# Late modulation weights of an adaLN block: other rooms for them, and their loads earlier in SyncE's list

## The chip, the cores and the metric

One core of a Trainium2 chip runs the whole program in one launch. The metric is the device time of the core in microseconds. TensorE (PE) multiplies, VectorE (DVE), ScalarE (ACT) and GpSimd (POOL) do the elementwise work, and SyncE (SP) issues nearly all DMAs. Each engine works through its own list of instructions in order; an instruction that has to wait holds up all that stand behind it on that engine.

## The reference, cut to what matters

```
mod = silu(c) @ w_mod                      # 640 -> 6 x 640: sa, ca, ga, sb, cb, gb
h = layernorm(x) * (1 + ca) + sa
x = x + ga * S4(h)                         # kernel of 2048 taps from the SSM parameters, FFT convolution, + h * Dskip
h = layernorm(x) * (1 + cb) + sb
x = x + gb * SwiGLU(h)                     # w1, w3: 640 x 1728, w2: 1728 x 640
```

x is 2048 x 640. The matrix `w_mod` has 3840 columns. The first 1920 (sa, ca, ga) are needed early, for the input and the kernel of the convolution. The last 1920 (sb, cb, gb) are the **late modulation weights**: their results are first used after the convolution.

## The kernel before, in words

The program has three parts. A **front** (the first 120 us or so) computes the SSM parameters, the early modulation, the layer norm of all 16 row tiles of x and the first step of the convolution's transform of the input (called u). Then **rounds** generate the convolution kernel for 40 groups of channels and run the rest of the transforms. Then the two branches of the **SwiGLU** run as large matrix products.

The front is ordered by a table of words written by hand, `FRONT`. Each word is one step, and the engines receive their instructions in the order of the words; the steps are kept in that order on each engine. The words that matter here:

- `um+j`: PE transforms row tile j into two tiles of PSUM. The first of them, with tag Z, is the only one of its kind.
- `ua+j`, `ub+j`: DVE (or ACT, with `/s`) copies the two halves into the SBUF tile `u` of row tile j. There are two such tiles, so `ua+15` (or `ub+14`, the first of its pair for row tile 14) writes where row tile 13 (or 12) was, and has to wait until that one is stored.
- `us+j`: SP stores tile `u` to DRAM, 128 rows of 1280 numbers, 640 KB. `us+12` is the thirteenth store.
- `wl+i`: SP loads late modulation weights i, 384 columns, 960 KB, in one or two DMAs.
- `qs+i`: PE multiplies them, in a PSUM tile with tag Z; `qp+i`, `qc+i`, `qv+i` bring the result into place (`mod_part`, `late_turn`, `late_cols`).
- `ul+0`: SP loads the first part of u back from DRAM. It waits for all stores of u.

In the order of the table, `qs+0` stands behind `ua+15`, since both use the PSUM tile with tag Z.

The five loads go into **rooms**: pieces of the large tile `uk` that hold other things at other times. `uk` has three planes of 4096 numbers per partition. `w_room(f, i, n, pitch)` gives the room that begins at number `i * pitch` of plane f, so each plane has two rooms for late weights, (f, 0) and (f, 1). Before, plane 0 holds the SSM parameters (`prm`: A, B, C, later their products), plane 2 holds temporary values of the same computation (`ldt`, `dt`, `m0` in its first room; `t3`, `gr`, `gi` and `l2` in its second). The steps of that computation on channels 128 to 639 are the words `d0` to `dN`; the last that touch the rooms are `dM`, `dN` (the phase, from `m0` and two of the products), `dA` (`dt` and `t3`) and `dB` (A's imaginary part and `t3`), all on DVE, and `dK` on PE (`l2`).

All loads and stores named here are issued by SP through one queue. Beside what a DMA's data needs, SP waits before it for the completion of the DMA that used the same completion semaphore before; eight such semaphores (`DMAHW0` to `DMAHW7`) take turns.

## Time and profile before

| | us |
|---|---|
| three runs | 929.12 median (928.58 to 930.3) |
| the profiled execution | 927.25, of which the span 925.5 |
| busy in the span: PE, DVE, ACT, POOL | 887.9, 698.9, 548.6, 265.9 |

The granted TensorE clock is 1.00 in all 40 slices of the span. The span is the time from the first to the last instruction of the profiled execution; 1.75 us of its run lie outside. PE is busy for 96% of the span, DVE for 76%. The change lies between 88 us and 121 us, in the last quarter of the front; what an engine waits for there has to be read from that stretch.

### The profile page before, as it was taken

What the parts mean: (1) busy time and instruction counts of PE and PEld (TensorE: products, weight loads), DVE (VectorE), ACT (ScalarE), POOL (GpSimd) and SP (SyncE); (2) the same over time, 40 slices, a digit from 0 to 9 for tenths busy, and PEclk for the clock granted to TensorE, in tenths of its full rate; (3) what the DMA queues carried; (4) which work ended last, traced back from release to release, by engine and by line L of the source; (5) the groups of instructions that cost most, each with busy time, mean ns of one, the idle gap of its engine ahead of it and who ended that gap; (6) DMA issues with size and microseconds to landing.
All of it is one profiled execution on the core that took longest, in us unless ns stands there. A gap on an engine that the chain in (4) does not pass through costs nothing.

```text
span 925.5 us, 21047 instructions
## 1 busy us (share of the span) xinstructions
PE 887.9 (96%) x8461; PEld 692.2 (75%) x8461; DVE 698.9 (76%) x1250; ACT 548.6 (59%) x811; POOL 265.9 (29%) x278
## 2 busy tenths in 40 slices
PE   5999889999999998999999999999999999999998
PEld 3776567777777666678888887778888888888886
DVE  6799888999999967876666655686976666664665
ACT  4899899999999743564343323556633333333432
POOL 3633454445446330243222201210522222100000
PEclk9999999999999999999999999999999999999999
DMA  8755898655656887942131217974322211103452
GB/s 254 258 202 192 272 226 216 176 161 157 178 159 174 200 264 213 261 176 86 57 111 60 58 44 217 278 234 153 95 64 71 85 58 57 58 29 100 150 177 101
DMA packets 103765, 140.68 MB, mean 152 GB/s; under 512 B 20212, under 2 KB 62964, under 8 KB 103668
## 3 DMA queue, kind: packets, MB, share of 16 engines
q1 hardware_dynamic: 100108, 129.48, 46.9%
q0 software_dynamic: 2048, 7.34, 2.4%
q10 hardware_dynamic: 1512, 2.52, 0.8%
q8 instruction: 66, 1.08, 0.5%
q14 instruction: 31, 0.25, 0.1%
HBM read 107.85 MB, written 31.46 MB: 151 GB/s over the span
## 4 chain that ended last, share of the span: by engine, by line
PE 67%; ACT 14%; DVE 12%; DMA 4%; issue 2%; SPq 0%; POOL 0%; DVEq 0%; ACTq 0%; POOLq 0%
PE ps L111 58%; ACT A L145 3%; PE p L676 3%; ACT ph L145 2%; ACT cs L145 2%; DVE E L597 2%; ACT L145 2%; DVE uk L111 2%; PE pm L111 1%; DVE A L604 1%; ACT kc L148 1%; PE pt L637 1%; DVE E L600 1%; ACT uk L148 1%; DMA A<-zs 1%
## 5 line engine op out<-in xcount | busy, mean ns | idle before, releaser
L111 DVE TENSOR_TENSOR s<-ps,s 128x512 f32<-128x512 f32 x138 | 95.0, 688 | 80.1 <-PE ps L111 79.8
L570 POOL TENSOR_TENSOR ph<-thi,iota 128x1024 int32<-128x1024 int32 x40 | 86.0, 2150 | 142.3 <-DVE A L608 94.9
L111 DVE TENSOR_TENSOR gl<-rw,gh 128x640 fp32r<-128x640 f32 x87 | 78.1, 897 | 64.3 <-ACT gh L111 64.3
L111 ACT CAST gh<-rw 128x640 fp32r<-128x640 f32 x87 | 63.2, 727 | 100.4 <-PE ps L111 62.6
L111 PE MATMUL ps<-xA,gh 128*128 128x512 f32 x280 | 88.5, 393 | 0.1
L111 PE MATMUL ps<-gh,uh 128*128 128x512 f32 x224 | 87.5, 390 | 0.0
L111 PE MATMUL ps<-gl,uh 128*128 128x512 f32 x224 | 87.2, 389 | 0.0
L111 POOL TENSOR_TENSOR S<-rw 128x256 f32<-128x256 f32 x46 | 36.5, 795 | 174.1 <-DVE S0l L111 163.1
L676 PE MATMUL p<-uk,s 128*64 128x256 f32 x640 | 77.9, 385 | 6.8 <-DVE Y L701 2.4
L111 PE MATMUL ps<-gh,ul 128*128 128x512 f32 x208 | 81.1, 390 | 0.0
L676 PEld LDWEIGHTS p<-uk,s 128*64 128x64 f32 x640 | 44.6, 136 | 29.5 <-DVE Y L701 3.5
L111 PEld LDWEIGHTS ps<-xA,gh 128*128 128x128 f32 x280 | 52.2, 188 | 13.6 <-issue 1.0
L111 PE MATMUL ps<-xA,gl 128*128 128x512 f32 x140 | 54.5, 390 | 0.0
L604 DVE TENSOR_TENSOR A<-A,ph 128x1024 f32<-128x1024 f32 x40 | 51.8, 1295 | 0.0
L111 ACT ACTIVATE s<-ps 128x512 f32<-128x512 f32 (+1 forms) x33 | 19.7, 597 | 53.1 <-PE ps L111 53.1
L597 DVE TENSOR_TENSOR E<-A,cs 128x1024 f32<-128x1024 f32 x40 | 50.2, 1254 | 0.6 <-ACT A L145 0.6
L111 PEld LDWEIGHTS ps<-gl,uh 128*128 128x128 f32 x224 | 42.1, 188 | 9.0
L111 PEld LDWEIGHTS ps<-gh,uh 128*128 128x128 f32 x224 | 42.1, 188 | 8.8
L111 PEld LDWEIGHTS ps<-gh,ul 128*128 128x128 f32 x208 | 39.0, 188 | 8.4
L574 POOL TENSOR_TENSOR ph<-ph,phi 128x512 int32<-128x512 int32 x40 | 44.5, 1115 | 2.5
L727 PE MATMUL pz<-Y,i 64*128 64x128 f32 x640 | 44.4, 278 | 0.7 <-ACT h L148 0.4
L727 PEld LDWEIGHTS pz<-Y,i 64*128 64x128 f32 x640 | 38.9, 187 | 7.1 <-issue 5.8
(251 smaller groups left out, 2287.8 us busy)
## 6 DMA issues: line engine op xcount, KB each, us to landing
rw<-in_w_dram SPq DMA_DIRECT2D x52, 320.0 KB, 2.9
us<-u SPq DMA_DIRECT2D x16, 640.0 KB, 3.2
s<-in_s_dram SPq DMA_DIRECT2D x40, 256.0 KB, 4.8
i<-in_i_dram SPq DMA_DIRECT2D x40, 256.0 KB, 3.3
rw<-in_wg_dram SPq DMA_DIRECT2D x31, 320.0 KB, 3.9
rw<-in_wu_dram SPq DMA_DIRECT2D x28, 320.0 KB, 2.8
uk<-us SPq DMA_DIRECT2D x32, 256.0 KB, 4.6
zs<-zt SPq DMA_DIRECT2D x16, 512.0 KB, 4.8
```

Of the source, the lines that this page charges most:

```text
L111: ins = fn(*args, **kw)
L145: return tc.keep_in_program_order(S.activation(*args, **kw))
L148: return tc.keep_in_program_order(S.copy(out, in_))
L570: keep(G.tensor_tensor(p, bc(thi[:, s * SD:s * SD + SD], 2, NPH), bc(iota, 1, SD), op=OP.mult))
L574: keep(G.tensor_tensor(p[:, :, :NA], p[:, :, :NA], bc(phi[:, s * SD:s * SD + SD], 2, NA), op=OP.add))
L597: keep(V.tensor_tensor(EC[s][:, :, 1:3, :], AA[s][:, :, 1:3, :], mid(cs[s]), op=OP.mult))
L600: keep(V.tensor_tensor(EC[s][:, :, 0, :], AA[s][:, :, 0, :], cs[s][:, :, 2 * NA - 1:NA - 1:-1], op=OP.mult))
L604: keep(V.tensor_tensor(A[:, :, 1:3, :], A[:, :, 1:3, :], mid(ph[s]), op=OP.mult))
L637: keep(PE.matmul(pt[c * 64:c * 64 + 64, g, :], kk[:, g, :], s1[:, c, :], start=True, stop=True, tile_position=(0, c * 64)))
L676: keep(PE.matmul(p2[par * 64:par * 64 + 64, pi, c, :], s2[:, pi * 2 + par, c * 64:c * 64 + 64], uk[:, 0:kn + 1:kn, f, :], start=True, stop ...
L727: ins = keep(PE.matmul(pz[:, par, (g % 2) * 2 + pi, :], i1[r, pi, c, :], Y[r, pi, c, :], start=(c == 0), stop=(c == 1), tile_position=(par ...
```

## The change

`late_load` gets another table of rooms. Loads 1 and 3 exchange their rooms: load 1 goes to (0, 1) where it was (2, 1), load 3 to (2, 1) where it was (0, 1). Loads 0, 2 and 4 keep theirs. In the table, `wl+0` and `wl+1` move in front of `us+12`, and also in front of the step `dB`; `wl+2` moves in front of `us+13`; `wl+3` moves from behind `um+15` to right behind `us+13`; `wl+4` stays.

```diff
-        wl[i] = w_load(w_room(0 if i in (2, 3) else 2, i % 2, WC, 2048), 1920 + i * WC)
+        wl[i] = w_load(w_room(*((2, 0), (0, 1), (0, 0), (2, 1), (2, 0))[i], WC, 2048), 1920 + i * WC)
...
-        "uk+0 ub+11/s dJ PI+7 kg+4 ua+11/s us+10 lg+7 dK/2 dN ln+12 lv+7 dA dH AB+7 um+12/A E1+6 dL us+11 dB "
-        "ua+12/s pt+2 SI+6 A1+5 uk+2 ub+12 us+12 K+4 um+13/B/2 ub+13 ua+13 ln+15 E2+5 ln+14 A1+6 wl+0 CO+7 "
+        "uk+0 ub+11/s dJ PI+7 kg+4 ua+11/s us+10 lg+7 dK/2 dN ln+12 lv+7 dA dH AB+7 um+12/A E1+6 dL us+11 wl+0 wl+1 dB "
+        "ua+12/s pt+2 SI+6 A1+5 uk+2 ub+12 us+12 wl+2 K+4 um+13/B/2 ub+13 ua+13 ln+15 E2+5 ln+14 A1+6 CO+7 "
```

This is the piece of SP's list that differs. The first row kept on both sides belongs to `us+10`, the second to `us+11`; the other rows `us<-u` are `us+12` and `us+13`; a row `uk<-in_w_mod_dram` is one DMA of a late load (384 columns: loads 0 and 4; 96 and 288: load 1; 192 twice: load 2; 288 and 96: load 3). In brackets stands what SP waits for.

```order
 L111 DMA us<-u 128x1280 [waits DMAHW0_49,DVE_49,Activation_49]
 L111 DMA us<-u 128x1280 [waits DMAHW1_49,Activation_49]
-L111 DMA us<-u 128x1280 [waits DMAHW2_49,DVE_49,Activation_49]
-L111 DMA uk<-in_w_mod_dram 128x5x384 [waits DMAHW3_49,Pool_49]
-L111 DMA us<-u 128x1280 [waits DMAHW4_49,DVE_49]
+L111 DMA uk<-in_w_mod_dram 128x5x384 [waits DMAHW2_49,DVE_49,Pool_49]
+L111 DMA uk<-in_w_mod_dram 128x5x96 [waits DMAHW3_49]
+L111 DMA uk<-in_w_mod_dram 128x5x288 [waits DMAHW4_49]
+L111 DMA us<-u 128x1280 [waits DMAHW5_49,DVE_49,Activation_49]
+L111 DMA uk<-in_w_mod_dram 128x5x192 [waits DMAHW6_49]
```

Between `us+11` and `us+12` there is now load 0 and load 1, three DMAs, and between `us+12` and `us+13` load 2, two DMAs, where load 0 stood. Load 0 now waits for DVE itself.

On DVE no instruction moves. This is the piece of its list around the evictions of row tiles 14 and 15; the rows `u<-pu,shift` with a change are `ub+14` and `ua+15`, which wait for the stores of row tiles 12 and 13.

```order
-L111 TENSOR_TENSOR u<-pu,shift 128x640 [waits DMAHW2_49,PE_49]
+L111 TENSOR_TENSOR u<-pu,shift 128x640 [waits DMAHW5_49,PE_49]
 L111 TENSOR_TENSOR u<-pu,shift 128x640
 L625 TENSOR_TENSOR pk<-pk,dz 128x4 [waits PE_49]
...
-L111 TENSOR_TENSOR u<-pu,shift 128x640 [waits DMAHW4_49,PE_49]
+L111 TENSOR_TENSOR u<-pu,shift 128x640 [waits DMAHW0_49,PE_49]
```

The same two stores are waited for; only their semaphores are others, since the stores stand at other places in SP's list. PE, ACT and POOL keep their instructions and their order too.

## Rows read from the trace of the kernel before

**Rows 1.** The page's chain of work that ended last, shares by engine

```profile
PE 67%; ACT 14%; DVE 12%; DMA 4%; issue 2%; SPq 0%; POOL 0%; DVEq 0%; ACTq 0%; POOLq 0%
```

**Rows 2.** Pieces of that chain, 93 to 116 us: start us, us, what

```profile
97.70 7.38 DMA us<-u
...
105.17 0.84 DVE u L111
...
106.05 1.02 PE pm L111 x16
...
113.69 0.45 PE pq L556 x4
...
114.15 0.93 ACT A L145 x2
```

**Rows 3.** Waits, 90 to 150 us: engine, line, releaser: total us, times, longest

```profile
ACT A L145 <- PE pa L545: 2.6, 3, 1.3
...
DVE u L111 <- DMA us<-u: 1.9, 1, 1.9
...
PE pm L111 <- DVE u L111: 1.5, 1, 1.5
```

**Rows 4.** SP's timeline, 85 to 122 us: start us, us, what SP issued

```profile
88.95 0.32 SPq L111 DMA_DIRECT2D us<-u  x1
...
95.77 0.32 SPq L111 DMA_DIRECT2D us<-u  x1
96.19 0.57 SPq L111 DMA_DIRECT2D uk<-in_w_mod_dram  x1
97.70 0.33 SPq L111 DMA_DIRECT2D us<-u  x1
...
104.81 2.05 SPq L111 DMA_DIRECT2D uk<-in_w_mod_dram  x1
...
110.63 1.89 SPq L111 DMA_DIRECT2D us<-u  x2
121.08 1.31 SPq L111 DMA_DIRECT2D uk<-us  x2
```

**Rows 5.** Windows: stretch, its us, five engines' busy us, clock, DMA share, GB/s

```profile
91.50:96.50 5.00, 4.26 (x52) 3.15 (x54) 4.93 (x9) 5.00 (x8) 2.55 (x1) 1.00 0.02 5
96.50:98.10 1.60, 1.14 (x18) 0.91 (x14) 1.60 (x3) 1.19 (x2) 1.25 (x2) 1.00 0.97 362
98.10:102.30 4.20, 3.58 (x90) 2.22 (x88) 4.17 (x8) 3.29 (x3) 2.11 (x1) 1.00 0.95 226
102.30:104.00 1.70, 1.70 (x56) 1.04 (x58) 1.01 (x2) 1.52 (x2) 0.72 (x2) 1.00 1.05 426
104.00:105.00 1.00, 0.59 (x44) 0.43 (x32) 0.00 (x0) 0.99 (x2) 1.00 (x1) 1.00 1.12 328
105.00:107.00 2.00, 0.95 (x17) 0.42 (x17) 0.82 (x1) 2.00 (x3) 2.00 (x3) 1.00 1.09 360
107.00:110.50 3.50, 3.50 (x38) 2.96 (x34) 3.30 (x7) 2.21 (x3) 0.37 (x1) 1.00 1.10 336
113.00:115.50 2.50, 2.47 (x30) 1.91 (x34) 2.11 (x4) 1.99 (x4) 0.92 (x1) 1.00 1.08 371
```

**Rows 6.** DMA packets by size, in 98.1 to 102.3 us, then 104 to 105

```profile
DMA packets 599, 0.95 MB, mean 226 GB/s; under 512 B 16, under 2 KB 584, under 8 KB 599
...
DMA packets 644, 0.33 MB, mean 328 GB/s; under 512 B 594, under 2 KB 634, under 8 KB 643
```

**Rows 7.** DVE's timeline, 88 to 106 us: start us, us, instruction

```profile
90.01 0.68 DVE L111 SCALAR_TENSOR_TENSOR uk<-uk 128x512 f32<-128x512 f32 x1
...
94.86 0.82 DVE L111 TENSOR_TENSOR u<-pu,shift 128x640 f32<-128x640 f32 x1
...
100.64 1.54 DVE L111 TENSOR_TENSOR u<-pu,shift 128x640 f32<-128x640 f32 x2
```

**Rows 8.** PE's timeline, 127.5 to 130 us: the first matmuls that read u back

```profile
128.03 1.95 PE L676 MATMUL p<-uk,s 128*64 128x256 f32 x16
```

## Prediction

> **What bounds the kernel now.** I read the chain that ended last first. PE holds 67% of it, ACT 14%, DVE 12%, and DMA only 4% [rows 1]. A change that touches nothing but SP's list can move the time only where a DMA is in that chain, so next I read the pieces of the chain around the moved loads. One DMA stands there: a store of u that SP issued at 97.70 and that took 7.38 us to land, at 105.08 [rows 2]. It is `us+13`: DVE's eviction `ua+15` starts right behind it, at 105.17, and the first late product `qs+0` at 106.05, when that eviction has freed its PSUM tile. From there PE runs on to 114.14 and hands over to ACT [rows 2].

> The table of waits says how much each engine lost there: DVE waited 1.9 us for the store, PE 1.5 us for DVE, and ACT at most 1.3 us at a time for PE [rows 3]. So if the store landed early enough, 1.3 us is about what could be gained, for then another engine is late; every microsecond that it lands later is lost in full, since the chain behind it has no gap. The late weights themselves are not in the chain: no wait of PE for a load appears.

> Why does the store need 7.38 us? SP's timeline, the rates by stretch and the packet sizes answer that together. SP issued `us+12` at 95.77, load 0 at 96.19, `us+13` at 97.70 [rows 4]. The DMA engines were idle from 91.5 to 96.5 (5 GB/s), then busy without a pause [rows 5]. The packets show whose bytes moved when: from 98.1 to 102.3 nearly all are between 512 B and 2 KB, the 1536 B rows of load 0; from 104.0 to 105.0 594 of 644 are under 512 B, the 384 B rows of load 1's first part [rows 6]. So the queue is served in order: `us+12` for 1.6 us, load 0 for 4.2, `us+13` for 1.7 (ending at 104.0), load 1's parts for 1.0 and 2.0 [rows 5]. The store landed 1.08 us after its last data.

> **The change part by part.** No instruction is added or removed on any computing engine; five loads keep their bytes. What changes is what stands in the queue ahead of `us+12` and `us+13`. Ahead of `us+13` there was load 0 (983 KB) and `us+12`; now there are loads 0, 1 and 2 (2,949 KB) and `us+12`. In return the queue may start earlier. The sum, on the profiled execution's clock:

> *Start.* Load 0 waits for DVE's last use of its room, the instruction at 90.01, done at 90.69 [rows 7]; SP is free from 89.27 [rows 4]. From issue to first data `us+12` took 0.73 us (95.77 to 96.5), so load 0 would begin at 91.4, and `us+11` has left the queue at 91.5. I take 91.5. The exchange of rooms costs nothing by itself: it only lets load 1 start without waiting for `dB`, whose temporaries lie in its old room. Three issues of about 0.6 us each fit before `us+12` is ready at 95.68, when `ub+12` is done [rows 7].

> *Loads 0 and 1.* Load 0 took 4.2 us at 226 GB/s in its row; load 4, of the same shape, moved at 371 GB/s, where 983 KB take 2.65 us [rows 5]. Which of the two will hold is not shown; load 0 again follows directly on a store, which speaks for the slow one, but the slow row has a reason that I can't name. I take the middle, 3.4, and keep both ends. Load 1 takes 3.0 by its own rows. It ends at 97.9 (97.15 to 98.7).

> *`us+12`.* So the queue is not free at 96.5, when this store's data moved before. It follows at 97.9 and ends at 99.5; with 1.08 it lands at 100.6 (99.8 to 101.4). `ub+14` wanted it at 100.64 [rows 7]: at worst 0.7 us late. DVE's 1.9 and PE's 1.5 us of waiting come behind it and hide that; without them it would cost 0.7.

> *Load 2.* 983 KB in 768 B rows. At 336 GB/s, the row in which these packets moved [rows 5], 2.9 us; ends 2.65 and 4.2 as for load 0, and it follows on a store like load 0 did. I take 3.4 and have 102.9.

> *`us+13`.* SP must first issue load 2. Late in the stretch, when the queue is full, an issue of 640 rows took 2.05 us instead of 0.57 [rows 4]; with two of that length the store would be issued at about 100.2, still before its turn in the queue. Data for 1.7, ending at 104.6, landing at 105.7. Before it was 105.08: **0.6 us later**. The low ends give 97.15 + 1.6 + 2.65 + 1.7 + 1.08 = 104.2, 0.9 earlier; the high ends 98.7 + 1.6 + 4.2 + 1.7 + 1.08 = 107.3, 2.2 later.

> *What comes free behind it.* Load 3 stands behind `us+13` as loads 1 and 2 did before, and lands near 109; load 4 has to wait for `qs+0` in its room and is late by the same 0.6. The last two stores, issued at 110.63 before, and landed when the load back began at 121.08 [rows 4], now have only load 4 ahead of them. By the same rates they land near 115.5, about 5 us earlier, and the load back can start when `qs+2` has read its room, near 117. This gives nothing: the first matmul that reads u back ran at 128.03 with no gap before it [rows 8]; it only waited its turn on PE.

> [...] The rows for loads read 226 to 371 GB/s here.

> The sum is 927.25 + 0.6 = 927.9 on the profiled execution. That run lies 1.9 us below the median of the runs, whose excess I can't place; on the median the forecast is 929.12 + 0.6 = **929.7 us**.

> **The rivals.**

> *Slow reads twice (slower).* Load 0 and load 2 each follow a store, and the one load seen in that place ran at 226 GB/s. If both do, the store lands 2.2 us later, at 107.3, and the chain behind it passes that on: 931.3. For it: the row itself. Against: every other load row is at 328 to 371. It decides once the store lands 1.86 us or more later than before.

> [...] If the transfers ran like the stores, 426 GB/s [rows 5], loads 0 and 1 would need 4.6 us and be done at 96.1, load 2 would need 2.3, and `us+13` would land at 96.5 + 1.6 + 2.3 + 1.7 + 1.08 = 103.2. Of the 1.9 us only about 1.3 is gained, where ACT becomes the bound: 927.8. Against it: no load row is that fast.

> *A larger wait than this execution shows (faster).* The runs lie 1.9 us above the profiled one. If that is a longer wait for `us+13` in other executions, or a wait for the load back, which comes about 5 us earlier now, the change could remove it and a part of the 1.3 besides: some 2.5 us, 926.6. Nothing in the trace shows such a wait, and the order of the queue speaks against the first.

> *Nothing changes* would hold if load 0 were issued no earlier than before. The list excludes it: it waits for DVE at 90.69 and stands ahead of `us+12`.

> **How the numbers follow.** The forecast 0.47, slow reads 0.25, all hidden 0.13, the larger wait 0.15. About 0.2%, 1.86 us here, is what a measurement of this kernel can tell from no change. The forecast's own range is 928.2 to 931.0; nearly all of it and the hidden case are within 0.2%: 0.56. Slow reads and the upper edge of the forecast are slower: 0.29. The larger wait is faster: 0.15. The range reaches from near the larger wait to beyond the slow reads: 926.8 to 932.0.

> **What would show it.** Right: in the profile after, the DMA engines carry over 200 GB/s from about 91.5 to 96.5; the packets up to 98 are those of loads 0 and 1; DVE still waits for a store of u before `ua+15`, and that store lands between 104.2 and 107.3; the load back begins near 117 instead of 121.08; the first matmul that reads u is late by what `qs+0` is late. Wrong: a start of load 0 well behind 91, a store `us+13` that lands before 104 (the queue would not be served in order, or faster than any load row), PE waiting for a late load, or a difference in the total that the start of `qs+0` doesn't show. If the time falls by more than 1.3 us, there was a wait that I haven't seen.

## The result: 0.4% slower, and the profile after

| | before | after |
|---|---|---|
| median of 22 runs each, us | 930.33 (927.85 to 941.66) | 933.93 (931.11 to 944.27) |
| ratio after/before, 95% interval | | 1.0042 (1.0023 to 1.0062) |
| span of the profiled execution, us | 925.5 | 932.2 |

The forecast was 929.7 with a range up to 932.0; the kernel became 3.6 us slower than before. The two profiled executions differ by more, 6.7 us, and a part of that lies where the change isn't. So first the places of the same events in both:

| us from the span's start | before | after | later |
|---|---|---|---|
| DVE starts the pair that ends in `ub+13`, ahead of all that the stores hold up | 96.12 | 97.27 | 1.15 |
| `ua+15` | 105.17 | 108.17 | 3.00 |
| first matmul that reads u back | 128.03 | 132.38 | 4.35 |
| the `ps<-idle` products, in the rounds | 369.81 | 376.64 | 6.83 |

About 1.0 of the first 1.15 us comes from a group of 16 dummy products at 23 us, long before any moved load: it takes 2.74 us before and 3.76 after, and between 2.66 and 3.78 in the other traces, whichever of the two kernels they start from. I take the 1.15 us off: from here on **times in front of the bar are counted from the start of the `ub+13` pair**. Then `ua+15` is 9.05 before and 10.90 after, the first matmul that reads u back 31.91 and 35.11. These 3.2 us are the loss of the stage. They come from one execution of each kernel; the medians differ by 3.6.

The chain of waits of the changed kernel, pieces from 97 to 113 us, answers to [rows 2]:

```profile
99.52 8.55 DMA us<-u
...
108.17 0.84 DVE u L111
...
109.05 1.83 PE pm L111 x16
110.88 1.56 PE pt L637 x16
```

The store `us+13` still ends the wait. But behind `ua+15` the late product `qs+0` takes 1.83 us where it took 1.02. The waits from 90 to 150 us, against [rows 3]:

```profile
ACT A L145 <- PE pa L545: 5.8, 3, 4.2
DVE u L111 <- DMA us<-u: 3.5, 1, 3.5
...
PE pm L111 <- DVE u L111: 3.1, 1, 3.1
```

SP's timeline of the changed kernel, against [rows 4]:

```profile
91.92 2.31 SPq L111 DMA_DIRECT2D uk<-in_w_mod_dram  x3
96.88 0.33 SPq L111 DMA_DIRECT2D us<-u  x1
97.25 2.17 SPq L111 DMA_DIRECT2D uk<-in_w_mod_dram  x2
99.52 0.67 SPq L111 DMA_DIRECT2D us<-u  x1
...
120.50 1.31 SPq L111 DMA_DIRECT2D uk<-us  x2
```

Loads 0 and 1 are issued at 91.92, as soon as DVE is done with the room, and the stores stand behind them. The load back starts at 120.50, or 119.35 on the clock of before, where 117 was forecast. The windows of the changed kernel (columns as in [rows 5]) tell the rest:

```profile
91.50:93.00 1.50, 1.50 (x32) 0.89 (x26) 1.43 (x4) 1.50 (x3) 0.00 (x0) 1.00 0.71 272
93.00:99.00 6.00, 4.78 (x61) 3.46 (x57) 5.93 (x10) 5.67 (x8) 3.80 (x2) 1.00 0.99 298
...
101.00:104.00 3.00, 2.13 (x72) 1.54 (x76) 2.82 (x6) 2.05 (x3) 2.29 (x1) 1.00 1.05 312
104.00:106.00 2.00, 1.99 (x82) 1.24 (x66) 0.70 (x2) 1.98 (x2) 1.16 (x1) 1.00 1.06 411
106.00:108.00 2.00, 0.00 (x0) 0.00 (x0) 0.00 (x0) 1.99 (x3) 2.00 (x3) 1.00 1.05 342
108.00:112.00 4.00, 2.95 (x28) 1.79 (x30) 1.88 (x3) 2.42 (x3) 0.75 (x1) 0.57 0.19 55
112.00:115.00 3.00, 3.00 (x28) 2.34 (x24) 2.93 (x6) 0.33 (x1) 0.00 (x0) 1.00 0.85 220
```

From 106 to 108 PE and DVE both do nothing. From 108 to 112 the granted clock is 0.57 (before it was 1.00 throughout), and PE's timeline shows what that costs (in brackets the idle time ahead):

```profile
109.05 1.83 PE L111 MATMUL pm<-uk,scb 128*32 128x384 f32 x16 [3.07 <-DVE u L111]
110.81 1.63 PE L637 MATMUL pt<-s,K 128*64 128x128 f32 x16
...
132.38 1.95 PE L676 MATMUL p<-uk,s 128*64 128x256 f32 x16
```

Before, these two groups took 1.02 and 1.09 us. The sum closes: 1.85 us of later landing, 0.81 for the slower `qs+0` and 0.54 for the slower `pt+3` are 3.20, and the first matmul that reads u back, against [rows 8], is 3.20 later.

### The profile page after: what moved, and what is told of

The parts are those of the page before. It is cut to its first block, busy times and chain, and to the rows that moved or that the text cites. A ratio compares the mean times of both kernels' runs of the same rounds, so it can differ in the third digit from the quotient of the medians.

```text
span 932.2 us, 21047 instructions
## 1 busy us (share of the span) xinstructions
PE 890.7 (96%) x8461; PEld 694.9 (75%) x8461; DVE 698.4 (75%) x1250; ACT 548.3 (59%) x811; POOL 265.8 (29%) x278
## 3 DMA queue, kind: packets, MB, share of 16 engines
q8 instruction: 66, 1.08, 0.5%
## 4 chain that ended last, share of the span: by engine, by line
PE 68%; ACT 14%; DVE 10%; DMA 4%; issue 2%; SPq 0%; ACTq 0%; DVEq 0%; POOLq 0%; POOL 0%
PE ps L111 58%; PE p L676 3%; ACT A L145 3%; ACT ph L145 3%; ACT cs L145 2%; PE pm L111 2%; DVE E L597 2%; ACT L145 2%; DVE uk L111 1%; PE pt L637 1%; PE pz L727 1%; DMA A<-zs 1%; ACT uk L148 1%; ACT kc L148 1%; DMA us<-u 1%
## 5 line engine op out<-in xcount | busy, mean ns | idle before, releaser
L145 ACT ACTIVATE A<-pa 128x1024 f32<-128x1024 f32 x40 | 41.5, 1038 | 5.9 <-PE pa L545 5.8
```

Source lines behind the costliest of these rows:

```text
L145: return tc.keep_in_program_order(S.activation(*args, **kw))
```

## The experiments

Two theories stood at the start. **Landing and clock**: the store lands later than forecast, PE's longer gap lets the granted clock fall, and both add up. **Landing only**: all of the loss is lateness. When the landing itself proved too late, two causes were set against each other: traffic in the queue, or a **code load** beside the store's last rows, which is my name for a packet of 16 KB in the queue that the page lists as `q8 instruction` (66 packets, 1.08 MB). The one in question began at 104.51 and took 1.00 us before, 105.96 and 1.03 us after. Whose instructions it carries isn't shown; that they are PE's was an assumption of mine, and so was that the packet holds up a DMA engine or PE.

All numbers at a glance, from one profiled execution each; "gap" is PE's idle time just before `qs+0`, or, marked s, a stall in which it waited for nothing that the profile shows. Medians of before were 930.3 to 931.9 in the different sets.

| kernel | `ua+15` | gap | `qs+0` | `pt+3` | first read of u | median | ratio (95%) |
|---|---|---|---|---|---|---|---|
| before | 9.05 | 1.46 | 1.02 | 1.09 | 31.91 | 930.33 | |
| after | 10.90 | 3.07 | 1.83 | 1.63 | 35.11 | 933.93 | 1.0042 (1.0023-1.0062) |
| e0_again | 10.48 | 2.56 | 1.80 | 1.94 | 34.98 | 933.52 | 1.0023 (0.9997-1.0049) |
| e1_rooms | 8.88 | 1.29 | 1.02 | 1.09 | 31.94 | 930.64 | 0.9988 (0.9969-1.0007) |
| e2_one | 7.11 | s 0.85 | 0.99 | 1.09 | 31.17 | 930.79 | 0.9981 (0.9959-1.0002) |
| e3_two | 7.28 | s 1.18 | 0.99 | 1.09 | 31.68 | 931.52 | 0.9995 (0.9974-1.0016) |
| e4_dummies | 10.63 | filled | 1.02 | 1.09 | 35.15 | 935.55 | 1.0046 (1.0028-1.0063) |
| e5_dummies9 | 10.71 | 0.30 | 1.02 | 1.09 | 33.57 | 936.47 | 1.0042 (1.0019-1.0065) |
| e6_hold | 13.07 | 5.47 | 1.83 | 1.98 | 44.63 | 937.98 | 1.0065 (1.0036-1.0094) |
| e7_quiet | 10.76 | 2.94 | 1.81 | 1.92 | 35.25 | 932.80 | 1.0017 (0.9995-1.0039) |
| e8_fetch_early | 8.95 | s 2.16 | 1.02 | 1.09 | 32.73 | 938.20 | 1.0064 (1.0039-1.0090) |
| e9_fetch_late | 10.60 | 2.14 | 1.49 | 1.97 | 35.02 | 933.80 | 1.0016 (0.9990-1.0043) |
| e10_hold2 | 11.08 | 3.49 | 1.83 | 1.98 | 39.34 | 935.08 | 1.0038 (1.0012-1.0063) |
| e11_one_fetch_early | 7.11 | s 1.61 | 1.02 | 1.09 | 32.18 | 934.76 | 1.0017 (0.9996-1.0039) |
| e12_late_pk | 10.70 | 4.11 | 1.83 | 1.53 | 37.40 | 937.13 | 1.0062 (1.0040-1.0083) |
| e13_one_fetch_late | 7.11 | none | 0.99 | 1.09 | 30.53 | 929.99 | 0.9991 (0.9970-1.0011) |
| e14_half | 8.76 | none | 0.98 | 1.09 | 32.97 | 931.20 | 1.0011 (0.9995-1.0028) |

The totals don't follow the stage alone: from the first read of u to `ps<-idle` these executions need 241.8 (before) to 250.8 us (e11_one_fetch_early), with waits for the rounds' own DMAs there. A stage that is 1 us better or worse is read from the stage.

**e0_again**: the changed kernel once more.

> The changed kernel once more. Queue theory: the store us+13 lands late because loads 0, 1 and 2 stand ahead of it in SP's queue (ua+15 starts 9.3 us or so behind the end of ua+13, 7.5 in the kernel before), PE then idles some 3 us ahead of qs+0, and its granted clock falls to 0.5 for about 3 us behind that, which costs 1.3 us more: together 3 to 4 us over the kernel before. Rival (chance): the low clock and the late store were accidents of one execution; then this profile shows neither, and the total is within 2 us of the kernel before.

Landing 10.48, gap 2.56, both products slow again: the loss of the stage, 3.07 us, repeats. The total of this set, 1.0023 (0.9997 to 1.0049), can't be told from no change.

**e1_rooms**: before, with the new rooms alone.

```diff
-        wl[i] = w_load(w_room(0 if i in (2, 3) else 2, i % 2, WC, 2048), 1920 + i * WC)
+        wl[i] = w_load(w_room(*((2, 0), (0, 1), (0, 0), (2, 1), (2, 0))[i], WC, 2048), 1920 + i * WC)
```

> The kernel before with the new rooms alone, all loads at their old places. Queue theory: no difference (within 1 us); ua+15 starts about 7.5 us behind the end of ua+13, the clock stays at 1.0. Rival (rooms): the exchange of rooms itself costs something, by writes into a plane that DVE or PE still uses; then 2 us or more are lost here too.

31.94 against 31.91: the rooms cost nothing. Its PE rows also show that behind a gap of 1.29 us the late product takes 1.02 us, as before:

```profile
107.58 1.02 PE L111 MATMUL pm<-uk,scb 128*32 128x384 f32 x16 [1.29 <-DVE u L111]
```

**e3_two and e2_one**: two loads, and one, ahead of `us+12`, none ahead of `us+13`.

```diff
 e3_two, against the changed kernel
-"... us+12 wl+2 K+4 ... us+13 wl+3 ub+14 ..."
+"... us+12 K+4 ... us+13 wl+2 wl+3 ub+14 ..."
 e2_one, against before (with the new rooms)
-"... dL us+11 dB ... A1+6 wl+0 CO+7 ..."
+"... dL us+11 wl+0 dB ... A1+6 CO+7 ..."
```

> The changed kernel with load 2 behind us+13 instead of ahead of it: loads 0 and 1 still ahead of us+12. Queue theory: us+13 has 983 KB less ahead of it, lands 2.5 to 3 us earlier than in the changed kernel, so 0.5 to 1 us earlier than in the kernel before; no long gap of PE, clock 1.0; total 0 to 1.3 us below the kernel before. Rival (us+12): the loss comes from us+12 standing behind loads 0 and 1, which is unchanged here; then 3 us are still lost.

> The kernel before with load 0 alone moved ahead of us+12; loads 1 to 4 at their old places, behind us+13 and later. Queue theory: load 0 is through before us+12 is ready, us+13 lands at its normal pace, near 101 on the clock of the kernel before, DVE doesn't wait for it; ua+15 starts 7.3 us behind ub+13 instead of 9.05, as in the run with two loads early. The gain that reaches the first matmul that reads u back is 0.2 to 1.3 us. Rival: a load ahead of us+12 costs something by itself; then no gain.

In both `us+13` lands before DVE wants it: `ua+15` waits for no DMA and starts 1.8 and 1.9 us earlier than before. Yet only 0.2 and 0.7 us reach the first read of u, and it isn't ACT that takes the rest, as the prediction had it, but PE itself (e2_one):

```profile
106.36 0.99 PE L111 MATMUL pm<-uk,scb 128*32 128x384 f32 x16
108.20 1.09 PE L637 MATMUL pt<-s,K 128*64 128x128 f32 x16 [0.85 <-issue]
```

**e4_dummies and e5_dummies9**: the changed kernel with 18 and with 9 dummy products into a free PSUM tile just before `qs+0`.

```diff
-"... XA+8 qs+0 qp+0 ..."
+"... XA+8 gap/18 qs+0 qp+0 ..."        # e5_dummies9: gap/9
```

> The changed kernel with 18 more dummy products of the identity on PE (2.5 us) right ahead of qs+0, in a PSUM tile that is free, so that PE is busy while it waits for ua+15. Queue and clock theory: the store lands as late as in the changed kernel, but the clock stays at 1.0, qs+0 and the products behind it take 1.0 us each again instead of 1.8 and 1.6; total 1.3 us below the changed kernel, about 2 us over the kernel before. Rival (the store alone): the clock costs nothing that counts, and the total is that of the changed kernel or, by the dummies, more.

> The changed kernel with 9 dummy products on PE ahead of qs+0. In the run with 18 they took 4.3 us, 1.7 us longer than the wait that they were to fill; 9 take about 2.2. Queue and clock theory: the store is as late as in the changed kernel (ua+15 starts 10.5 to 10.9 us behind the start of ub+13, 9.05 in the kernel before), PE idles under 1 us ahead of qs+0, the clock stays at 1.0, and the first matmul that reads u back starts 33.5 us behind ub+13 instead of 35.1 (31.9 in the kernel before). Rival (the store alone): it stays at 35.

A dummy product is two matmuls in the rows. 18 were too many: they ran until 1.7 us behind the end of `ua+15`, and what the clock gave back they took. 9 fit. The store is as late as in the changed kernel, but PE's gap is 0.30 us and the two products take 1.02 and 1.09 us, as before:

```profile
105.52 2.27 PE L111 MATMUL pa<-ident 128*128 128x128 f32 x18
108.09 1.02 PE L111 MATMUL pm<-uk,scb 128*32 128x384 f32 x16 [0.30 <-DVE u L111]
109.04 1.09 PE L637 MATMUL pt<-s,K 128*64 128x128 f32 x16
```

The first read of u is at 33.57, 1.5 us earlier than in the changed kernel and 1.66 later than before. So 1.5 of the 3.2 us belong to the clock: landing only is out. The total did not follow. In the profiled execution the rounds took 250.3 us instead of 241.8, with 3.0 and 2.2 us of PE waiting for the DMA `A<-zs`; why the median of all 12 runs, 936.47, shows no gain either is open.

**e6_hold and e10_hold2**: before, with three and with two extra DVE operations on a dead tile ahead of `ua+15`; no DMA moves.

```diff
-"... um+15/B kg+6/1 wl+2 ua+15 ..."
+"... um+15/B kg+6/1 wl+2 hold ua+15 ..."
```

> The kernel before, loads and rooms untouched, with three DVE operations of 1.2 us on a tile that nobody needs any more ahead of ua+15, so that ua+15 starts some 1.8 us later than it would, as in the changed kernel, with the queue as it was. Theory of the clock: PE idles about 3.2 us ahead of qs+0, its clock falls to 0.5 behind that, qs+0 and the products of pt+3 take 1.8 and 1.6 us instead of 1.0 each, and the first matmul that reads u back starts 35 us behind ub+13 (31.9 before): 1.8 us of waiting cost 3.1. Rival (the fall of the clock belongs to the DMA traffic or to the execution, not to PE's idling): the clock stays at 1.0 and it starts at 33.7.

> The kernel before with two extra DVE operations on a dead tile ahead of ua+15 (the hold with three overshot: 6.04 us of work). No DMA is moved. ua+15 starts at 11.1 after ub+13, about 2.1 later than before, PE's gap before qs+0 is about 3.4 us. Theory clock (a gap of PE that long is followed by a granted clock of 0.5): qs+0 and the pt step behind it take 1.8 and 1.6 to 1.9 instead of 1.02 and 1.09, and the first matmul that reads u back is 3.3 to 3.8 later than before, at 35.2 to 35.7. Rival (the clock fell for the DMA traffic, or the loss is only the lateness): 2.1 later, 34.0.

Three held `ua+15` up by 4.0 us, too much for a comparison; two by 2.03, about what the changed kernel has. The products fell to 1.83 and 1.98 us as expected, but the loss is 7.4 us, not the 3.3 to 3.8 expected. Windows of e10_hold2:

```profile
104.00:106.00 2.00, 0.83 (x60) 0.67 (x48) 1.97 (x2) 1.99 (x3) 2.00 (x1) 1.00 1.07 326
106.00:108.00 2.00, 0.00 (x0) 0.00 (x0) 2.00 (x2) 1.04 (x2) 2.00 (x2) 0.68 1.09 371
108.00:112.00 4.00, 3.68 (x33) 2.18 (x33) 2.02 (x6) 2.34 (x2) 1.44 (x2) 0.50 1.10 330
112.00:120.00 8.00, 8.00 (x44) 5.50 (x42) 3.74 (x7) 3.04 (x4) 0.00 (x0) 0.50 0.93 335
120.00:122.00 2.00, 2.00 (x17) 1.53 (x19) 2.00 (x3) 0.16 (x1) 0.23 (x1) 0.91 0.02 8
```

**e7_quiet**: the changed kernel, load 3 behind load 4, so that nothing follows `us+13` in the queue.

```diff
-"... us+13 wl+3 ub+14 ... qv+1 wl+4 XA+10 ..."
+"... us+13 ub+14 ... qv+1 wl+4 wl+3 XA+10 ..."
```

> The changed kernel with load 3 behind load 4, so that nothing follows us+13 in the queue until qs+0 has run; what stands ahead of it is unchanged. In the changed kernel the last large packet of us+13 ended about 1.8 us before the store counted as landed, 0.6 to 0.9 in the kernel before. Theory of the traffic behind it: with an empty queue behind it the store lands within 1 us of its last packet, ua+15 starts 9.6 us behind ub+13, and PE's clock may stay up; total about 1 to 2 us below the changed kernel. Theory of the traffic ahead of it: the same 1.8 us, ua+15 at 10.5 or later, total as in the changed kernel.

`ua+15` at 10.76: the traffic behind isn't the cause. The queue now drains, and the DMA rows show the end of the store alone, first from 105.0 to 105.25, where the code load begins, then from 105.5 to 107.25 (the DMA row: busy share in 40 slices):

```profile
DMA packets 19, 0.07 MB, mean 291 GB/s; under 512 B 7, under 2 KB 7, under 8 KB 18
...
q8 instruction: 1, 0.02, 25.1%
```

```profile
DMA  0000000000000700000000000300002000000000
GB/s 0 0 0 0 0 0 0 0 0 0 0 0 0 117 0 0 0 0 0 0 0 0 0 0 0 117 0 0 0 0 117 0 0 0 0 0 0 0 0 0
DMA packets 5, 0.02 MB, mean 9 GB/s; under 512 B 2, under 2 KB 2, under 8 KB 5
```

125 of the store's 128 rows have begun by 105.3; the last three begin one by one from 106.10 to 106.85, with two packets under 512 B as the only others from 105.5 to 107.25, and the store lands at 107.5. The code load is charged with 25.1% of 16 engines' 0.25 us, which is 1.0 us, from 105.11 to 106.11. The first of the three rows begins as it ends. That they were queued behind it was my guess, which no row shows; it made the second pair of theories.

**e8_fetch_early and e9_fetch_late**: before with 36 more, and the changed kernel with 36 fewer PE instructions around 64 us, to shift the code load against the store.

```diff
 e8_fetch_early (dummies of 64 columns where the number is over 20)
-"... pt+1/8 ... PA+6/A/7 ..."
+"... pt+1/33 ... PA+6/A/31 ..."
 e9_fetch_late
-"... pt+1/8 ... PA+6/A/7 ..."
+"... pt+1/3 ... PA+6/A/3 ..."
```

> The kernel before with nothing moved in SP's list. Two groups of dummy products around 64 us (8 and 7 of 128 columns) become 13 and 11 of 64 columns, so that PE has 36 more instructions to read (weight loads counted) and its code load (queue q8 in the DMA rows, one packet of 16 KB, 1.0 us of one DMA engine), which began at 104.5, 0.1 us behind the last row of us+13, begins about 1.2 us earlier, while rows of us+13 still move. Times are relative to the start of the pair ub+13. Theory code load (it holds up the store's rows on one DMA engine and with them the landing): the last rows come about 1 us later, ua+15 starts at 9.9 to 10.4 instead of 8.9 to 9.05, PE's gap before qs+0 grows to 2.2 to 2.8, and the first matmul that reads u back is at 32.8 to 34.5 instead of 31.9; +1 to +2.5 us on the whole. Rival traffic (the landing was late in the changed kernel for the loads ahead in the queue): nothing changes, ua+15 at 9.05, first matmul at 31.9, the time as before.

> The changed kernel with 9 dummy products fewer around 64 us (8 to 3, 7 to 3), so that the same code load, which began at 105.95 with the last row of us+13 at 106.95, begins about 1.2 us later, behind the store's last row. Theory code load: the last row moves near 8.9 after ub+13 and the store lands 0.7 us later, ua+15 starts at 9.4 to 9.8 instead of 10.5 to 10.9; PE's gap is 1.6 to 2.0, and the first matmul that reads u back is at 32.3 to 32.8 if the clock holds, 33.8 if it falls, instead of 35.0. The whole is 2 to 3 us faster than the changed kernel, about the time of before. Rival traffic: ua+15 at 10.5 to 10.9 and the first matmul at 35.0, as in the changed kernel.

Both miss. The code load began 8.0 after `ub+13` in the one and 8.3 in the other, against 8.4 before and 8.7 after. It did not move by the 1.2 us (executions of the changed kernel alone have it between 8.3 and 8.7), so they test nothing about the landing. They show two other things. In e8_fetch_early PE stands still for 2.16 us, and not at `pt+3` as in e2_one but some 36 instructions further up:

```profile
109.92 0.24 PE L622 MATMUL pk<-A 128*32 128x64 f32 x1 [2.16 <-issue]
110.04 1.02 PE L111 MATMUL pm<-uk,scb 128*32 128x384 f32 x16
```

And the length of a gap alone doesn't settle the clock: behind 2.14 us in e9_fetch_late it fell to 0.50 and `qs+0` took 1.49 us, behind the 2.16 us here it stayed at 1.00 and `qs+0` took 1.02.

**e12_late_pk**: the changed kernel, 66 products taken from ahead of `qs+0` to behind it, so that PE is much further back in its list while the store moves.

```diff
-"... um+15/B kg+6/1 ua+15 AB+8 SI+7 PH+10 XA+8 qs+0 qp+0 ..."
+"... um+15/B ua+15 AB+8 SI+7 PH+10 XA+8 qs+0 kg+6/1 qp+0 ..."
```

> The changed kernel with the pk products of kg+6 (66 matmuls, 1.6 us) behind qs+0 in PE's list instead of ahead of it; SP's list, and so the DMA queue, is the changed kernel's. While PE waits for ua+15 it is then some 130 instructions (weight loads counted) further back than in the changed kernel, so a code load that PE's progress asks for would come only behind the landing of us+13. Times after the start of ub+13. Theory code load: if it moves so, the last row of us+13 leaves near 8.9 and ua+15 starts at 9.4 to 9.8 instead of 10.5 to 10.9. If the code load stays at 8.2 to 8.7, ua+15 stays at 10.5 to 10.9, and it isn't PE's place in its list that asks for it. Rival traffic: the code load moves and ua+15 is at 10.5 to 10.9 all the same. PE's gap before qs+0 grows by the 1.6 us of the moved products, to 3 to 4.6 us, with a granted clock near 0.5 behind it; the whole is as slow as the changed kernel or up to 1.5 us slower.

The code load began at 8.5 all the same, and `ua+15` at 10.70. So its start didn't follow PE's place in the list here; the pair is still not parted.

**e14_half**: the changed kernel with the second half of load 2 behind `us+13`.

```diff
-"... us+12 wl+2 K+4 ... us+13 wl+3 ub+14 ..."
+"... us+12 wl+2 K+4 ... us+13 wm+2 wl+3 ub+14 ..."   # wl+2: 192 columns, wm+2: the other 192
```

> The changed kernel with only the first half of load 2 (192 of 384 columns, 491 KB) ahead of us+13 and the second half right behind it. Ahead of us+13 stand then 2,458 KB of loads and us+12, against 2,949 KB in the changed kernel and 983 KB before. By the changed kernel's own rows the store's data end some 1.4 us earlier, near 7.4 after the start of ub+13, about 1 us ahead of the code load at 8.2 to 8.7. Theory code load: it lands 0.7 us behind its last row as it did before, near 8.1; ua+15 starts at 7.8 to 8.4 (before 9.05, changed 10.5 to 10.9) and the first matmul that reads u back is at 31.2 to 31.7. Rival traffic (the landing runs 1.8 to 2 us behind the data once two to three loads stand ahead): ua+15 at 9.2 to 9.5, and the first matmul at 31.9 to 32.4.

The last large row left 7.84 after `ub+13`, 0.4 later than expected, and just then, at 7.75, the code load began. `ua+15`, at 8.76, falls between the two forecasts. DVE's row shows that the store was no longer what it waited for:

```profile
105.76 0.82 DVE L111 TENSOR_TENSOR u<-pu,shift 128x640 f32<-128x640 f32 x1 [0.40 <-PE pu L111]
```

The trace has its landing at 8.55, 7.0 us behind its issue and 0.7 us behind the start of its last row, as in the kernel before, with 2,458 KB of loads ahead of it. A tail from that amount of traffic ahead is out. The first read of u missed its mark (32.97 against 31.2 to 31.7): the store before it, `us+12`, was 1.08 us late for `ub+14`, PE idled 1.52 us for it, and the granted clock went down to 0.50 for the `pk` products.

**e11_one_fetch_early and e13_one_fetch_late**: e2_one with the same 36 instructions more, and fewer.

> The kernel with load 0 alone ahead of us+12, and the code load 1.2 us earlier by the same 36 instructions. There PE stood still for 0.85 us within the pt step, which began about 1.5 us behind the end of the code load. Theory code load (PE had run out of instructions): the stall goes or shrinks to under 0.2, and the first matmul that reads u back is at 30.2 to 30.8 instead of 31.17 after ub+13; the whole is 1 to 1.6 us faster than before, the best of all kernels here. Rival (the stall has another cause): the stall of 0.85 stays and the first matmul is at 31.2.

> The kernel with load 0 alone ahead of us+12, and 9 dummy products fewer around 64 us, so that the place in PE's list where it ran out of instructions (0.85 us within the pt step; 1.6 us and 36 instructions further up in the kernel with more dummies) lies 36 instructions further down, behind the pt step. Theory code load: there PE arrives some 1.3 us later, the code load has come meanwhile, the stall is gone or under 0.3, and the first matmul that reads u back is at 30.2 to 30.7 after ub+13 instead of 31.17 (before 31.91); the whole is 1 to 1.6 us faster than before. Rival (the stall is bound to the pt step or to the store's early landing): 0.85 of stall, first matmul at 31.2.

With more, the stall grew to 1.61 us and moved up to the same `pk` product as in e8_fetch_early, against what I expected (I had counted on an earlier code load). With fewer it is gone, as expected, and with it the whole cost:

```profile
105.21 0.99 PE L111 MATMUL pm<-uk,scb 128*32 128x384 f32 x16
106.14 1.09 PE L637 MATMUL pt<-s,K 128*64 128x128 f32 x16
```

The stall keeps its place in PE's list of instructions and meets other products when the list shifts. It ends 2.4 to 2.6 us behind the start of a code load (e3_two 105.16 and 107.55, e2_one 105.73 and 108.20, e8_fetch_early 107.30 and 109.92). What PE waits for there the traces don't show; that it had run out of instructions, as the expectations put it, was my assumption. e13_one_fetch_late has the best stage of all, 30.53 against 31.91, and the lowest median, 929.99; but 0.9991 (0.9970 to 1.0011) is no gain that could be told from none.

## Why the prediction was wrong

*Start, order, loads.* Right, with two small errors against each other. With the 1.15 us added, the first data were due at 92.65 and loads 0 and 1 through at 99.05. Load 0's first row moved at 93.3, and the first rows of `us+12` at 99.3: 6.0 us for the two loads instead of 6.4. Load 2 was to end at 104.05; its packets give way to the store's around 104.2. Neither the slow rival's 226 GB/s nor the stores' 426, which the hidden case took for the loads, appeared: loads 0 and 1 run at 298 GB/s, load 2 at 312.

*`us+13`: the term that failed first.* The prediction's step "Data for 1.7, ending at 104.6, landing at 105.7", and so its "0.6 us later". The data were nearly right: due to end at 105.75, and all of the 128 rows but one had begun by 106.14. The landing wasn't. It was due at 106.85 and came at 108.08, so the store was 1.85 us later than before. The 1.08 us from data to landing was misread, too: by its rows the store before ended at 104.42 and landed 0.66 us behind. The DMA rows from 106.15 to 107.05 have one packet over 2 KB, the row that is missing:

```profile
DMA packets 277, 0.32 MB, mean 355 GB/s; under 512 B 3, under 2 KB 276, under 8 KB 277
```

Where the 1.2 us went can be read in the traces. For each of these stores and loads they record sixteen completions (events on its semaphore), and its landing is the last of them: DVE started `ua+15` 0.09 us behind the sixteenth of `us+13` in both. Before, the fifteenth came at 104.87 and the sixteenth at 105.08. After, the fifteenth came at 106.79, where the forecast had the landing; the sixteenth came 1.28 us later. One completion of the sixteen was late, not the store as a whole.

It is late at the time at which a code load begins. In each of the 17 traces one begins 7.6 to 8.7 us after `ub+13`, and in 16 of them the distance from fifteenth to sixteenth completion jumps there from one DMA to the next, from at most 0.24 us to between 0.77 and 1.56. In ten of them the DMA that shows it is a load (before: load 1's first part, 1.35 us, right behind `us+13`); in six it is the store `us+13` (after, e0, e4, e5, e7, e12). In e9_fetch_late one completion was late already, and a second joins it. In the three traces with rows left over (after, e5, e7) the first of them begins within 0.02 us of the end of the code load, and in the seven traces with a landing at 10.4 to 10.8 the store lands 1.1 to 1.4 us behind that end. In before and e1_rooms the last row left 0.1 to 0.2 us ahead of the code load, and the landing took 0.65.

So traffic behind the store is excluded (e7_quiet), and the amount ahead as the cause of the late landing too (e14_half; before, where 983 KB ahead leave load 1 just as late). Of the 1.85 us, the three loads ahead cost 0.77: by so much the fifteenth completion is later than before. The other 1.07 are the sixteenth alone. What stays open is why: the trace doesn't name the DMA engine of a packet, and no experiment managed to move the code load. That it delays the store is not shown, only that the two fall together. In e8_fetch_early, e14_half and e10_hold2 it began 0.1 to 0.5 us ahead of the store's last row and the store landed 0.6 to 0.7 us behind that row all the same.

*"Every microsecond that it lands later is lost in full."* This step failed outright. 1.85 us cost 3.2: at PE's gap of 3.07 us its clock fell to 0.50 for 3.4 us, and the next products took 1.35 us longer. e5_dummies9 shows it with the same landing, e10_hold2 without any DMA.

*The cap on a gain.* "1.3 us is about what could be gained, for then another engine is late": the size is right (1.38 in e13_one_fetch_late), the engine wasn't. PE stood still with no releaser that the profile shows, and that took 0.85 (e2_one) and 1.18 us (e3_two) of it, until the place was moved.

*Load back near 117.* Wrong and harmless. Load 4 had to wait for `qs+0`, and the last two stores behind it were issued at 112.27, not by 110.6. The load back started at 120.50, and the first matmul that reads u back again only waited its turn, as forecast.

*The rivals.* The one on the slower side had the right sign and, by luck, nearly the right landing (2.2 us later; it was 1.85): the reads that it needed weren't slow, and its 931.3 still counted the lateness once.

In the stage, issuing one load earlier gained time (the first read of u at 31.17 in e2_one and 30.53 in e13_one_fetch_late, 31.91 before), and issuing three earlier lost it (35.11).

## What to carry to other kernels

Count what an early load puts ahead of a store that someone waits for: one or two loads of 983 KB fitted here (`ua+15` at 7.11 in e2_one and 7.28 in e3_two, 9.05 before), three did not (10.90). Price a longer wait of PE not by its length alone: look at the granted clock behind the gap (here 1.00 behind 1.46 us, 0.50 behind 3.07), and try dummy products in it where the wait can't be avoided (here they gave the stage 1.5 us back, and the total nothing). Where a DMA lands late behind its data, look whether all of its completions are late or one (here one of sixteen, 1.28 us behind the fifteenth). And when a wait goes and the gain doesn't arrive, look for a stall with no releaser on the engine itself (here 0.85 and 1.18 us).

## What the runs showed of the hardware that was not expected

- **Clock.** The length of a gap alone didn't decide. Gaps of PE of 1.29 and 1.46 us left the granted clock at 1.00, and so did stalls of 1.61 and 2.16 us (e11, e8) and a wait of 2.58 us in the rounds of e0_again; behind waits of 2.14 to 5.47 us ahead of `qs+0` it was 0.50, in e14_half already behind 1.52 us. It stayed low for 3.4 us (after) to 13.7 us (e10_hold2) and 20.5 us (e6_hold), with PE busy for most of that time.
- **Code loads.** The kernel before has 66 packets of 16 KB on the queue `q8 instruction`. A packet took 0.88 to 1.67 us, half of them under 1.04. Three stalls of PE, of 0.85 (e2_one), 1.18 (e3_two) and 2.16 us (e8_fetch_early), ended 2.4 to 2.6 us behind the start of one; with 36 PE instructions fewer, 40 us earlier, the 0.85 us were gone (e13_one_fetch_late), with 36 more they were 1.61 (e11_one_fetch_early).
- **Landing.** With nothing changed in the store, its sixteenth completion came 0.01 to 0.24 us behind the fifteenth in ten traces, and 0.97 to 1.35 us behind it in six of the seven where it landed late. Other DMAs that were in the queue when a code load began show the same: before, the four of loads 1 and 2 (1.25 to 1.39 us), after, the two of load 3 (1.12 and 1.21).
